# Between-products of all steps as 32x32x32 from the inverted blocks, and the first chunk's chain reordered without most fillers

## The chip, the cores and the metric

The kernel runs on one core of one Trainium2 chip. The metric is the device time of one execution, in microseconds. A core has TensorE (PE, with its weight loads shown apart as PEld), VectorE (DVE), ScalarE (ACT), GpSimd (POOL) and SyncE (SP), which here issues nearly all DMAs.

## The reference

A delta rule attention with 4 batches, 8 heads, 768 positions and head dimension 48, and behind it a feed-forward layer with a parametric ReLU.

```python
k_n = k / (norm(k) + 1e-06)
for t in range(S):                       # state: (B, H, 48, 48), from zero
    y[:, :, t] = q[:, :, t] @ state
    v_old = state^T k_n[:, :, t]
    state += beta_t * outer(k_n[:, :, t], v[:, :, t] - v_old)
x = y as (B*S, H*D) = (3072, 384)
h = x @ w_in                              # (384, 2048)
g = max(h, 0) + alpha * min(h, 0)
return g @ w_out                          # (2048, 384)
```

## The kernel before

**Tiling.** The sequence is cut into 12 chunks of 64 positions. A step n (24 of them) is one chunk of one pair of batches: two batches lie in the two halves of the 128 partitions, 8 heads along the free axis. Within a chunk the recurrence becomes a triangular system: the Gram matrix of k (grams) gives a unit triangular 64x64 matrix per batch and head, whose inverse is applied to the right-hand side (solve). Then come the outputs, the next state (next_state), and the transposes into the feed-forward's input (to_ffn).

**The inverse by blocks.** A 64x64 triangular matrix has two 32x32 diagonal blocks and one 32x32 block between them. The diagonal blocks of four steps at a time (NJ = 4) are inverted by DVE (eliminate; for the first four steps eliminate_small, which goes to 16 and lets TensorE do the last doubling in cross). Their results are `inverse` and its transpose `turned`. The off-diagonal block of the inverse is a product of three: inverse block, off-diagonal block of the Gram matrix (in `right`), inverse block. These are the between-products: between_1 multiplies `right` by the turned first block into `mid`, between_2 multiplies `mid` by the second inverse block, and the result goes into `inv`, from which solve reads. Partitions 0 to 31 and 64 to 95 hold first blocks, 32 to 63 and 96 to 127 second blocks.

In the kernel before there are two forms, chosen by `changes(n)` (n > 4):
- Steps 0 to 4: products of 64x64 weights and 32 columns per batch and head. The blocks are first copied with a mask (`which`, one column per block) into zero-padded 64x64 tiles `diag`; `right` and `mid` carry zero columns as well. DVE adds the result of between_2 to the second block (L720).
- Steps 5 to 23: products of 32x32 weights and 32 columns. For half of the heads the output is put in the other half of the partitions (`quad(2 * (t ^ a) + 1)`), so consecutive products use four places of the array; this takes second blocks copied across the partition halves (two 64x128 copies). ScalarE copies the result.

`place`/`placing` make these copies, with parts 0 (first block, turned), 1 (second block), 2 (into inv) and 3 (two small copies of weights).

**Order.** The order of every engine's instructions is the program's order; nothing is rescheduled. The start goes: statics (norms and Gram matrices of steps 0 to 3), queries, zeros (memzero of padded tiles on ScalarE), fillers (`busy(n)`: 2n products of 512 columns or part of one, whose result nobody reads, L1388), the elimination on DVE beside them, then first_chunk (steps 0 and 1 with nothing else to do on TensorE), second_pair (steps 2 and 3, woven with the first feed-forward products, first_in), and from step 4 on a steady mix: attention's bursts (burst_a, burst_b), with feed-forward products (L929 first layer, L971, L993 and later L1246 second layer) woven between by `weave`. In burst_b of step n, between_2 of step n + 1 and between_1 of step n + 2 share a call from step 7 on.

**Weights.** They come as 64-bit words in pieces of 512 KB. `fetch` issues a piece's DMA on SP, `begin` starts its conversion on ScalarE (L225, L226), the `conv_in` generator ends it on DVE in two parts (L235, L240) and then lets the next piece be fetched into the freed space. There are 12 pieces of w_in and six spaces. `convert(n)` runs n parts; `ahead[0]` tells how far `begin` may run ahead.

Names in the text: cross is L593 (first stage), L603 and L610 (second stage, with the copy L598 between); place is L648 on ScalarE and L644 on DVE; between_1 is L682 (32-wide) and L693 (64-wide), between_2 L707 and L712; their copies L689, L698, L725; solve L786 and L790; outputs L799; next_state L815 and L823.

Of the kernel before, what the change touches and what calls it, by code (L numbers as in the profile page):

```python
# [32 lines left out]
C = 64  # L33
HB = 32
W_IN_P = 512
BUSY = 8
# [7 lines left out]
def kernel(  # L44
# [272 lines left out]
    diag = [const.tile([128, H, C], FP32, name=f"diag{i}") for i in range(NE)]  # L317
    inv = [const.tile([128, H, C], FP32, name=f"inv{i}") for i in range(NE)]
    mid = [const.tile([128, H, C], FP32, name=f"mid{i}") for i in range(2)]

    right = [const.tile([128, H + 1, HB], FP32, name=f"right{i}") for i in range(EARLY)]

    def zeros():

        for t in right:
            nc.scalar.memzero(t[:, 0])
        for t in mid + diag + inv + state:
            nc.scalar.memzero(t)
# [89 lines left out]
    def grams(n, p=None):  # L418
# [10 lines left out]
        def weighted(dst, cols):  # L429
# [7 lines left out]
            lambda: weighted(right[n % EARLY][:, 1:], slice(HB, C)),  # L437
# [29 lines left out]
    def keep(n):  # L467

        m, j = n // NJ, n % NJ
        for t in range(2):  # L470
            own = slice(64 * t + HB, 64 * t + C)
            if n < FIRST + NJ and n != NJ - 1:
                nc.gpsimd.tensor_copy(out=same[m][own, j], in_=right[n % EARLY][own, 1:])
            elif n < NJ and t == 0:
                nc.vector.tensor_copy(out=same[m][own, j], in_=right[n % EARLY][own, 1:])
            else:
                nc.scalar.copy(same[m][own, j], right[n % EARLY][own, 1:])
# [144 lines left out]
    CROSS = 2  # L622

    def changes(n):

        return n > NJ

# [4 lines left out]
    def placing(n, parts, by_vector=False):  # L632
# [5 lines left out]
        first, second = slice(0, HB), slice(HB, C)  # L638

        def put(dst, cols, src, i, rows=slice(0, 128), to=None, a=slice(0, 2)):  # L640
            heads = slice(j * H + a.start * G, j * H + a.stop * G)
            out, x = dst[n % NE][to or rows, a.start * G : a.stop * G, cols], src[m][rows, heads]
            if by_vector:
                nc.vector.tensor_scalar(  # L644
                    out=out, in0=x, scalar1=which[rows, i : i + 1], scalar2=None, op0=ALU.mult
                )
            else:
                nc.scalar.mul(out, x, which[rows, i : i + 1])  # L648

        if 0 in parts:  # L650
            put(diag, first, turned, 0)
            yield
        if 1 in parts:
            put(diag, second, inverse, 1, a=slice(0, 1 if changes(n) else 2))
            yield
            if changes(n):
                for t in range(2):
                    put(diag, second, inverse, 1, half(t), half(1 - t), slice(1, 2))
                    yield
        if 2 in parts:  # L660
            put(inv, first, inverse, 0)
            yield
            if changes(n):
                put(inv, second, inverse, 1)
# [1116 lines left out]
```

## Time and profile before

| | |
|---|---|
| timed runs | 666.43, 671.92, 672.93 us, median 671.92 |
| profiled execution | 668.2 us, its span 666.5 |
| TensorE busy | 641.1 us (96%) |
| TensorE weight loads | 565.8 us (85%) |
| VectorE busy | 492.5 us (74%) |
| ScalarE busy | 288.6 us (43%) |
| GpSimd busy | 93.2 us (14%) |
| mean granted TensorE clock | 0.995 |

In the lines of the profile, a timeline row is start, length, engine, line, operation, written tile and read tiles, shape and count, and in brackets the idle time before it and what ended it. A row of the chain of waits is start, length, what. In the table of stages, each row is a stretch of time, its length, then for each of PE, PEld, DVE, ACT and POOL the busy time with the number of instructions, then the granted TensorE clock, the share of the DMA engines and GB/s. An fp32 product shows as two TensorE instructions. One between-call of a step is 16 products, so 32 instructions.

### The profile page before, as it was taken

What the parts mean: (1) busy time and instruction counts of PE and PEld (TensorE: products, weight loads), DVE (VectorE), ACT (ScalarE), POOL (GpSimd) and SP (SyncE); (2) the same over time, 40 slices, a digit from 0 to 9 for tenths busy, and PEclk for the clock granted to TensorE, in tenths of its full rate; (3) what the DMA queues carried; (4) which work ended last, traced back from release to release, by engine and by line L of the source; (5) the groups of instructions that cost most, each with busy time, mean ns of one, the idle gap of its engine ahead of it and who ended that gap; (6) DMA issues with size and microseconds to landing.
All of it is one profiled execution on the core that took longest, in us unless ns stands there. A gap on an engine that the chain in (4) does not pass through costs nothing.

```text
span 666.5 us, 22184 instructions
## 1 busy us (share of the span) xinstructions
PE 641.1 (96%) x9551; PEld 565.8 (85%) x9551; DVE 492.5 (74%) x1181; ACT 288.6 (43%) x675; POOL 93.2 (14%) x201
## 2 busy tenths in 40 slices
PE   4989999999998999999999999999999999999997
PEld 4577787666687998998998998998999999999997
DVE  5955889878989869748949747859869658568383
ACT  5837755336556343444434433324235345142140
POOL 6000121001010000001000000000035044053260
PEclk9799999999999999999999999999999999999999
DMA  8947754211332032122021022111112210100000
GB/s 121 243 120 200 192 115 120 72 36 32 68 74 49 11 65 50 21 53 49 15 49 36 15 48 37 20 44 36 27 37 38 37 36 5 25 14 2 24 1 25
DMA packets 110962, 37.72 MB, mean 57 GB/s; under 512 B 104160, under 2 KB 107248, under 8 KB 110864
## 3 DMA queue, kind: packets, MB, share of 16 engines
q1 hardware_dynamic: 109088, 35.81, 24.8%
q8 instruction: 75, 1.23, 0.8%
q10 hardware_dynamic: 1776, 0.49, 0.4%
q14 instruction: 23, 0.19, 0.1%
HBM read 31.56 MB, written 4.72 MB: 54 GB/s over the span
## 4 chain that ended last, share of the span: by engine, by line
PE 75%; DVE 15%; ACT 5%; issue 2%; SPq 2%; DMA 1%; POOL 0%; DVEq 0%; ACTq 0%; POOLq 0%
PE p_ffn L993 17%; PE p_ffn L929 16%; PE p_more L1246 8%; PE p_more L1161 4%; PE p_ffn L1151 3%; PE p_ffn L1246 3%; PE p_ffn L1156 2%; DVE prod L516 2%; DVE block L522 2%; PE p_pair L377 2%; PE p_pair L786 2%; DVE act L941 2%; PE p_pair L761 2%; PE p_pair L1388 2%; PE p_pair L799 2%
## 5 line engine op out<-in xcount | busy, mean ns | idle before, releaser
L929 PE MATMUL p_ffn<-xt,w_in 128*128 128x256 f32 x768 | 175.4, 383 | 5.0 <-ACT sums L939 1.8
L929 PEld LDWEIGHTS p_ffn<-xt,w_in 128*128 128x128 f32 x768 | 142.4, 190 | 26.3 <-ACT sums L939 2.2
L941 DVE SCALAR_TENSOR_TENSOR act<-act,al_t,p_ffn 128x256 f32<-128x256 f32 x112 | 48.6, 475 | 28.7 <-ACT act L939 28.6
L939 ACT ACTIVATE act<-p_ffn 128x512 f32<-128x512 f32 x56 | 33.3, 595 | 77.1 <-PE p_ffn L929 76.9
L522 DVE TENSOR_TENSOR block<-block,prod 128x30 f32<-128x30 f32 (+9 forms) x150 | 49.9, 333 | 5.1
L1185 POOL TENSOR_TENSOR k_t<-k_t 128x128 f32<-128x128 f32 (+1 forms) x48 | 29.6, 616 | 166.2 <-ACT k_t L1180 163.7
L516 DVE TENSOR_TENSOR prod<-block 128x30 f32<-128x30 f32 (+9 forms) x150 | 48.8, 326 | 3.3 <-POOL block L506 1.6
L993 PE MATMUL p_ffn<-w_out,act 128*128 128x192 f32 x288 | 49.6, 328 | 0.2 <-DVE act L941 0.2
L840 ACT COPY xt<-p_pair 128x384 f32<-128x384 f32 x22 | 10.4, 477 | 85.8 <-PE p_pair L838 73.6
L993 PEld LDWEIGHTS p_ffn<-w_out,act 128*128 128x128 f32 x288 | 46.5, 190 | 0.8 <-issue 0.5
L366 POOL TENSOR_TENSOR beta_t<-beta_t,rec 128x8 f32<-128x8 f32 x24 | 6.3, 261 | 291.1 <-DVE rec L364 270.8
L1185 POOL TENSOR_TENSOR block<-block 128x128 f32<-128x128 f32 (+1 forms) x48 | 28.0, 583 | 16.3 <-ACT block L1180 13.8
L1151 PE MATMUL p_ffn<-xt,w_in 128*128 128x256 f32 x96 | 28.7, 380 | 0.0
L648 ACT ACTIVATE diag<-inverse,which 64x128 f32<-64x128 f32 (+2 forms) x60 | 24.3, 404 | 2.3 <-DVE inverse L489 1.3
L771 DVE TENSOR_TENSOR r<-v_raw,p_pair 64x192 f32<-64x192 f32 (+1 forms) x66 | 23.2, 352 | 1.1
L725 ACT COPY inv<-p_pair 32x256 f32<-32x256 f32 x38 | 13.7, 362 | 23.6 <-DVE u L790 23.4
L790 DVE TENSOR_TENSOR u<-p_pair,wgt 128x384 f32<-128x384 f32 x24 | 13.3, 557 | 14.2 <-PE p_pair L682 10.1
L1200 DVE SCALAR_TENSOR_TENSOR act<-block,al_t,act 128x256 f32<-128x256 f32 x32 | 19.1, 638 | 5.2 <-ACT block L1196 5.1
L349 DVE TENSOR_REDUCE norm<-ksq 128x8 f32<-128x384 f32 x24 | 13.0, 545 | 12.9 <-ACT ksq L347 12.9
L1013 DVE TENSOR_TENSOR o_sb<-u,p_ffn 128x192 f32<-128x192 f32 x24 | 7.9, 352 | 19.7 <-PE p_ffn L993 19.2
L1246 PE MATMUL p_more<-w_out,act 128*128 128x192 f32 x128 | 21.9, 329 | 0.0
L1180 ACT COPY k_t<-p_more 128x512 f32<-128x512 f32 x16 | 9.4, 586 | 28.7 <-PE p_more L1161 25.9
(223 smaller groups left out, 1417.5 us busy)
## 6 DMA issues: line engine op xcount, KB each, us to landing
w_out<-in_moe_w_in_dram SPq DMA_DIRECT2D x12, 512.0 KB, 5.4
qp<-in_q_dram SPq DMA_DIRECT2D x48, 96.0 KB, 3.0
v_raw<-in_v_dram SPq DMA_DIRECT2D x48, 96.0 KB, 2.9
kl<-in_k_dram SPq DMA_DIRECT2D x96, 48.0 KB, 2.6
out_dram<-o_sb SPq DMA_DIRECT2D x92, 48.0 KB, 1.6
space_out<-in_moe_w_out_dram SPq DMA_DIRECT2D x11, 384.0 KB, 3.8
ke<-in_k_dram SPq DMA_DIRECT2D x43, 96.0 KB, 3.2
w_out<-in_moe_w_out_dram SPq DMA_DIRECT2D x5, 384.0 KB, 5.0
```

Source lines behind the costliest of these rows:

```text
L516: nc.vector.tensor_tensor(out=prod, in0=r[:, 0:j, j : j + 1].to_broadcast([128, j, n]), in1=r[:, j : j + 1, j + 1 : HB].to_broadcast([128, ...
L522: nc.vector.tensor_tensor(out=r[:, 0:j, j + 1 : HB], in0=r[:, 0:j, j + 1 : HB], in1=prod, op=ALU.add)
L648: nc.scalar.mul(out, x, which[rows, i : i + 1])
L771: nc.vector.tensor_tensor(out=r[to, a], in0=v_in[to, a], in1=p[own, a, :, 0:D], op=ALU.subtract)
L929: nc.tensor.matmul(p_h[:, i], w_in[:, t, (f + i) * 128 : (f + i + 1) * 128], xt[:, t], start=(t == 0), stop=(t == KT - 1),)
L939: nc.scalar.activation(g, p_h, ACT.Relu, scale=-1.0)
L941: nc.vector.scalar_tensor_tensor(out=g[:, i], in0=g[:, i], scalar=al_t[:, f + i : f + i + 1], in1=p_h[:, i], op0=ALU.mult, op1=ALU.add,)
L993: nc.tensor.matmul(p, x(i), w(i), start=(i == 0), stop=(i == FP - 1))
L1151: nc.tensor.matmul(p[:, f * 256 : f * 256 + 256], w(2, f), xt[:, 2], start=True, stop=False)
L1161: nc.tensor.matmul(q[:, j], a, b, start=True, stop=True)
L1185: nc.gpsimd.tensor_tensor(out=dst, in0=a, in1=b, op=ALU.add)
L1246: nc.tensor.matmul(p, x(i), w(i), start=(i == 0), stop=(i == FP - 1))
```

## The change

- All steps use 32x32x32 products. The first product goes from first-block rows to second-block rows of PSUM, the second from second-block to first-block rows, with no swap of halves. So a call that stands alone alternates between two places of the array; where between_2 of one step and between_1 of the next share a call, their products alternate head by head.
- between_1 reads `turned` itself for steps 0 to 3, and from step 4 a plain copy of it in `diag`; between_2 reads the second block out of `inv`. The masked copies into `diag`, the copies across halves, and the zero columns of `right`, `mid` and `diag` with their zero writes are gone. The result of between_2 is always copied, not added.
- placing yields 3 pieces instead of 6 (PLACING).
- statics: the transposes of step 0 (flips) go ahead of betas; weigh(0) ahead of squares(1).
- BUSY is 6 instead of 8; begin_in takes 5 pieces instead of 4 ahead of the elimination.
- first_chunk is rewritten: cross is written out with its two sums in banks of their own, one filler of 0.75 and one of 0.5 are left, placements and half of the copies go to DVE, and the masks, weight conversions, next-state updates and loads stand in another order: the loads of later k and v now come before the conversion of pieces 3 to 5.

```diff
-BUSY = 8
+BUSY = 6
...
-        for t in right:
-            nc.scalar.memzero(t[:, 0])
-        for t in mid + diag + inv + state:
+        for t in inv + state:
             nc.scalar.memzero(t)
...
+        own = slice(j * H, j * H + H)
+        def put(cols, i):
+            out, x = inv[n % NE][:, :, cols], inverse[m][:, own]
...
-        if 0 in parts:
-            put(diag, first, turned, 0)
+        if 0 in parts and n >= NJ:
+            nc.scalar.copy(diag[n % NE], turned[m][:, own])
             yield
         if 1 in parts:
-            put(diag, second, inverse, 1, a=slice(0, 1 if changes(n) else 2))
-            yield
-            if changes(n):
-                for t in range(2):
-                    put(diag, second, inverse, 1, half(t), half(1 - t), slice(1, 2))
-                    yield
+            put(slice(HB, C), 1)
+            yield
         if 2 in parts:
-            put(inv, first, inverse, 0)
-            yield
-            if changes(n):
-                put(inv, second, inverse, 1)
-                yield
+            put(slice(0, HB), 0)
+            yield
...
+    def turned_of(n):
+        return diag[n % NE] if n >= NJ else turned[0][:, n * H : n * H + H]
+
+    def products(n, second, p):
+        to, frm = (0, 1) if second else (1, 0)
+        x, y = (
+            (mid[n % 2], inv[n % NE][:, :, HB:C]) if second else (right[n % EARLY], turned_of(n))
+        )
+        def product(i, t):
+            rows = quad(2 * t + frm)
+            nc.tensor.matmul(p[quad(2 * t + to), i // G, i % G], x[rows, i], y[rows, i])
+        return product
+
+    def copied(n, second, p, vector=False):
+        to = inv[n % NE][:, :, HB:C] if second else mid[n % 2]
+        to = to.rearrange("p (a g) i -> p a g i", a=2)
+        def copies():
+            for t in range(2):
+                rows = quad(2 * t + (0 if second else 1))
+                if vector:
+                    nc.vector.tensor_copy(out=to[rows], in_=p[rows])
+                else:
+                    nc.scalar.copy(to[rows], p[rows])
+        return [copies]
+
+    def between(*wanted, vector=False):
...
+        for i in range(H):
+            for product in todo:
+                for t in range(2):
+                    product(i, t)
+        return [y for x in wanted for y in copied(*x, vector)]
...
-        soon += between_2(n + 1, b[:, :, WY : WY + G * HB])
+        wanted = [(n + 1, True, b[:, :, WY : WY + G * HB])]
         if n > JOINED:
-            soon += between_1(n + 2, b[:, :, 2 * WY : 2 * WY + G * HB])
+            wanted.append((n + 2, False, b[:, :, 2 * WY : 2 * WY + G * HB]))
+        soon += between(*wanted)
```

The new first_chunk from its second stage on, whole:

```diff
+        nc.scalar.copy(half_way[:, 0:bs, 0:LB], p)
+        begin_in(6)
+        busy(0.75)
...
+        for b in range(bs):
+            for i in (0, 2):
+                nc.tensor.matmul(
+                    one[quad(i), b], inverse[0][quad(i), b], half_way[quad(i), b, 0:LB]
+                )
+        for i in (0, 2):
+            y = turned[0][quad(i), 0:bs, 0:LB]
+            nc.vector.tensor_tensor(out=y, in0=y, in1=one[quad(i)], op=ALU.add)
+        for b in range(bs):
+            for i in range(4):
+                nc.tensor.matmul(
+                    two[quad(i), b], half_way[quad(i), b], inverse[0][quad(i), b, LB:HB]
+                )
+        scale_v(0)
+        y = inverse[0][:, 0:bs, LB:HB]
+        nc.vector.tensor_tensor(out=y, in0=y, in1=two, op=ALU.add)
         for i in both:
+            now(between_1(i, vector=i == 1))
+            place(i, (1,), True)
+        place(0, (2,))
+        place(1, (2,), True)
+        scale_v(1)
         for i in both:
+            now(between_2(i, vector=i == 1))
+        mask(0)
         for i in both:
             now(through_state(i))
             now(solve(i))
-        busy(0.5, ps_ffn())
+        mask(1)
+        busy(0.5)
         now(outputs(0))
+        state_of = [next_state(0)]
+        to_ffn(0, ps_ffn())
+        now(outputs(1))
+        state_of.append(next_state(1))
         convert(4)
+        to_ffn(1, ps_ffn())
+        convert(2)
         for i in both:
+            now(state_of[i])
             load_late(i + 2)
             load_v(i + 3)
+        convert(4)
         ahead[0] = FT * DM
         convert(2)
```

In second_pair the two calls of place(n, (0,)) are gone.

## The prediction

> **What bounds the kernel now.** I read the page's busy shares first, then the table of stages, the chain of waits up to 75 us, the timeline of the first 50 us, and last the rows of the between-product lines.
>
> ```profile
> PE 641.1 (96%) x9551; PEld 565.8 (85%) x9551; DVE 492.5 (74%) x1181; ACT 288.6 (43%) x675; POOL 93.2 (14%) x201
> 29.00:36.70 7.70, 7.52 (x331) 5.31 (x330) 5.61 (x15) 3.49 (x7) 0.00 (x0) 1.00 0.64 115
> 36.70:49.00 12.30, 10.30 (x333) 8.82 (x333) 6.93 (x16) 3.46 (x9) 0.00 (x0) 1.00 0.31 97
> 260.00:500.00 240.00, 239.77 (x3549) 220.47 (x3548) 178.19 (x437) 90.98 (x218) 11.14 (x25) 1.00 0.18 35
> ```
>
> From 260 to 500 us TensorE is busy for 239.77 of 240: there only TensorE work counts, and ScalarE (91 of 240) has slack. The first 49 us are different: TensorE is busy, but partly with products that compute nothing (L1388, the fillers), and those are on the chain that sets the end:
>
> ```profile
> 19.54 9.51 PE p_pair L1388 x16
> 29.04 1.33 PE p_pair L593 x89
> 30.37 1.06 PE p_pair L1388 x2
> 31.43 0.61 PE p_pair L603 x32
> 32.04 0.63 PE p_pair L1388 x2
> 32.67 0.61 PE p_pair L603 x32
> 33.28 0.63 PE p_pair L1388 x2
> 33.91 1.37 PE p_pair L610 x89
> ...
> 48.96 1.99 PE p_ffn L929 x8
> ```
>
> So 48.96, where the feed-forward products (L929) begin, is a chain's end, and every microsecond cut ahead of it is a candidate for the whole span. What DVE has ready, and when:
>
> ```profile
> 25.96 1.10 DVE L489 STREAM_TRANSPOSE turned<-block 128x256 f32<-128x256 f32 x2
> 26.92 2.22 DVE L489 STREAM_TRANSPOSE inverse<-block 128x256 f32<-128x256 f32 x4
> 36.18 0.42 DVE L619 TENSOR_TENSOR inverse<-inverse,p_pair 128x256 f32<-128x256 f32 x1
> 36.74 1.01 PEld L693 LDWEIGHTS p_pair<-diag,right 64*64 64x64 f32 x32 [0.41 <-ACT diag L648]
> 31.36 0.58 PEld L603 LDWEIGHTS p_pair<-act,inverse 32*32 32x32 f32 x32 [0.76 <-ACT act L598]
> 157.91 0.34 PEld L707 LDWEIGHTS p_pair<-diag,mid 32*32 32x32 f32 x32
> ```
>
> L593 could start at 27.06, when the turned blocks are there; the fillers hold it to 28.97. The last three rows are prices. A call is 32 instructions: 31.6 ns each for 64-wide products in two places of the array (L693), 18.1 for 32-wide ones with 16 columns in two places (L603), 10.6 for 32-wide ones with 32 columns in four places (L707).
>
> **What the skill says.** "TensorE: Matmul & The Clock Gate", Part 3, says that a weight load overlaps running products only where the row group differs. L707 uses two row groups, as L603 does, yet in four places it runs at 10.6 ns instead of 18.1; so I price by places. The same page, Part 1, describes a clock at half rate after an idle window of some 3.4 us and full after a busy one. The trace agrees in kind: 0.50 from about 17.2 to 24.3 us, after the idle stretch from 13.1 to 16.0, and 1.00 from then on. "ScalarE: Activation LUTs", What ACT_TABLE_LOAD costs, gives 186 ns + 0.833 ns per element, and 93 ns more for a per-partition operand: 492 for the masked 128x256 write, and the trace has 491 to 513 (L648). The plain copy that replaces one is then an estimated 400.
>
> **First chunk, step by step.** Times are of the profiled execution.
> Start: ScalarE drops 12 zero writes (right 1.05, mid 1.14, diag 1.14 = 3.3 us) and gets one weight piece more ahead of the chain (L225 + L226, 1.35), so it is free at 29.12 - 3.3 + 1.35 = 27.1. The pieces are there: the first six are issued between 14.76 and 17.94 and land within 8.4 us, by 26.3. The earlier transposes of step 0 can bring DVE forward by the wait for the step-0 Gram products, some 0.4 us at best; TensorE's fillers end later than that, so I count 0 (bounds -0.5 and 0).
> Fillers: BUSY 8 to 6 takes 4 products of 0.43: L593 at 27.25, ending at 28.6. In before the copy starts 1.68 after L593 does, so here it runs 28.95 to 29.3. The 0.65 us of filler left lies under that copy. The 64 products of "one" follow directly, 64 x 18.1 ns: 30.5 (before: 33.2, split by fillers). The 128 of "two" take 1.31: 31.8. DVE adds to turned 30.65 to 31.5 (L617, 2 x 0.42), scales v (0.55), and adds to inverse until 32.5. Before that was 36.60.
> Between-products: the new call has 32 instructions in two places with 32 columns. This isn't in the trace. From below L603's 18.1 ns (0.58 us), from above L693's 31.6 (1.01). L603 with 16 columns more, at the 0.84 ns per column of L1388 (0.43 us for 512), is 0.79 if nothing overlaps; I take 0.65. The first call for step 0 ends at 32.5, for step 1 at 33.2. Copies on ScalarE (2 x 0.365, L689) for step 0 end at 33.4; on DVE (2 x 0.42, as L617) for step 1 at 34.2, and step 1's inverse block, also by DVE, at 34.5. The second call for step 0 starts at 33.5, for step 1 at 34.6. ScalarE's copies end at 35.0, DVE's, behind two placements (0.35 each) and scale_v(1), at 36.25.
> Solve and output: DVE is now the slower side: mask(0) 0.75 to 37.0, u 2 x 0.56 to 38.1, mask(1) 0.75 to 38.9. The output products of step 0 run at 37.6, its y is copied by 38.8, its transposes wait for mask(1) (it reads both p_ffn banks); outputs(1) at 39.4, y by 40.6, transposes 40.65 to 41.1, xt copy 41.2 to 41.65. DVE converts three weight pieces (0.42 + 0.69 each) from 38.9 to 42.2, just ahead of the third product. So L929 starts at 41.7 for 48.96: -7.3 (bounds -5.0 and -8.5; a stall in TensorE's issue like the 0.59 ones at 37.9 and 45.7 would take part of it).
>
> **Second pair.** The first conversions end at 40.0 instead of 33.3, so weight pieces 6 to 8 are requested at 40 to 42.3, with 5.4 us to land. The last convert of the chunk puts piece 6 on ScalarE right after the xt copy at 41.65, where it waits for that landing until about 45; behind it stand squares(4), piece 7 and the two L598 copies, ready at some 48.6, and TensorE's L603 wants them at 41.7 + 6.8 = 48.5: just hidden, and each us that the landing is late is a us lost. SP then issues the 12 loads of k and v (10.2 us in before, 7.8 at 0.65 each) ahead of pieces 9 to 11, which before lay in front of the loads. Piece 9 lands at 56 to 58, L929's start plus 14.3 to 16.5. ScalarE wants it at plus 12, and in order behind it stand the L939 activations, the mid copies and the placements that the second between-call waits for (in before L712 waits there for ScalarE, 0.64 and 0.22). The two diag writes dropped (1.0) pay for the extra mid copies (1.46 for 0.62). ScalarE falls 2 to 4 us back, and has some 2 idle to win back: I take +1.5 on TensorE, less 0.3 for the shorter last product call: +1.2 (bounds 0 and +3.5).
>
> **Steps from 4 on.** Step 4: two calls at 0.65 for 1.01, -0.7. Calls that stand alone were in four places and now are in two: the first product of steps 5 to 8, the second of 5, 6, 7 and 23. Eight at 0.65 for 0.34: +2.5. In the 15 joint bursts the two calls alternate, so four places stay in turn: 64 instructions at 10.2 ns before (344.49 to 345.14) and after, 0 (bounds +-0.1 each). Sum +1.8 (bounds +0.8 and +5).
> ScalarE loses 0.40 + 0.81 + 0.1 us of placements in each of 19 steps, 25 us in all, beside TensorE work that hides it: I count -0.3 for L929's few waits on it (bounds -1 and 0). If that cover were missing it would be worth more, not less.
> Sum: -7.3 + 1.2 + 1.8 - 0.3 = -4.6 us. The profiled execution took 668.2 (span 666.5, 1.7 around it) and would take 663.6. The three timed runs are 666.43, 671.92, 672.93; the mean of all four is 670.0. The profiled one is no typical middle, so I subtract from the mean: 665.4.
>
> **The rivals.**
> A, the forecast: 665.4, chance 0.5.
> B, the head start is lost less: pieces 9 to 11 land in time and the two-place call costs 0.58. Then -7.3 + 0 + 0.8 - 1 = -7.5, 662.5. For it: DMA share is only 0.31 from 36.7 to 49. Against: SP issues in order. Chance 0.2.
> C, the gain is given back: the weight pieces land at the slow end, and two-place calls cost like L693: -5.5 + 3 + 4 = +1.5, 671.5; or an issue stall adds to the shorter chain. Chance 0.18.
> D, the other side: the clock. From 29.25 to 36.85 the new order has no full-array filler, 7.6 us of small products with gaps. If TensorE is throttled to half there, every microsecond of its work costs 0.5 to 1 more. Before, only a long filler stretch brought it back, and the next full-array stretch of over 5 us comes only after 90 us. It eats the 4.6 after some 10 us at half clock, and with 30 us at half clock it gives 670 - 5 + 15 = 680. For it: the half clock ended only within the fillers. Against: from 36.7 to 39.5 before, two products of 1.0 us with a 0.6 gap and no filler left it at 1.00. Chance 0.12.
>
> **How the numbers follow.** A and most of B and C give the range 659.5 to 671.5; the tail of D and a little of B are left out. About 1% (6.7 us) is what a measurement of this kernel can tell from no change. Below 665.2 lie B and almost half of A, 0.45; over 678.6 lies most of D, 0.1; the rest is 0.45.
>
> **What would show it.** Right: L593 near 27.2, L929's first near 41.7, clock 1.00 from 29 to 49, lone between-calls near 0.65 and joint bursts near 0.65 for 64. Wrong: a clock below 1.00 after 29 us; L929 starting after 44; a joint burst over 0.8; ScalarE waiting for a weight DMA between 50 and 60 us by more than 4 us.

## The result and the profile after

After takes 669.95 us (median of 19 executions, 667.72 to 671.85), before, on the same chip, 670.48 (19, 666.43 to 675.22). The ratio is 0.999 with the interval 0.9969 to 1.0011: no change that can be measured, where 665.4 was forecast. The profiled execution took 668.25 us, its span 666.5, to the tenth that of before.

Lines are renumbered: the first feed-forward products are L908 (L929 before), all between-products L671, their copies L686 on ScalarE and L684 on DVE, the placements L639 and L635, solve L765, outputs L778, next_state L794, the transposes into the feed-forward L817, the copy behind them L819, fillers L1368. The cross of the first chunk is L1402, then L1411 ("one") and L1419 ("two"). In kernels that keep before's first chunk on the new products the cross is L591, L601, L608.

The page's busy shares, and the three stages that were shown of before:

```profile
PE 642.7 (96%) x9535; PEld 569.2 (85%) x9535; DVE 494.3 (74%) x1180; ACT 263.1 (39%) x613; POOL 92.1 (14%) x201
29.00:36.70 7.70, 4.62 (x262) 3.81 (x264) 3.72 (x9) 2.85 (x6) 0.00 (x0) 0.88 0.50 90
36.70:49.00 12.30, 11.09 (x278) 9.19 (x275) 10.08 (x23) 2.83 (x7) 0.00 (x0) 0.52 0.36 106
260.00:500.00 240.00, 239.46 (x3550) 220.72 (x3549) 178.15 (x438) 78.67 (x191) 11.13 (x25) 1.00 0.18 36
```

ScalarE lost 25.5 us of work, as worked out. But in the first chunk TensorE, without the fillers, is busy for 4.62 of 7.70 us instead of 7.52, and from 36.7 on the granted clock is 0.52. The chain of waits through the chunk shows where the head start went:

```profile
26.54 1.10 DVE turned L487 x2
27.64 0.14 issue
27.78 1.39 PE p_pair L1402 x86
29.17 0.84 PE p_pair L1368 x2
30.01 1.08 PE p_pair L1411 x61
31.13 0.39 PE p_pair L1419 x38
31.51 0.80 issue
32.31 1.01 PE p_pair L1419 x62
33.33 0.71 PE p_pair L671 x44
34.04 2.28 issue
36.32 0.76 PE p_pair L671 x18
...
38.38 1.07 PE p_pair L671 x32
39.44 2.25 PE p_pair L765 x64
...
48.86 1.99 PE p_ffn L908 x8
```

Up to 31.5 the order does what was said. Then TensorE stops twice in the middle of a run of small products, 0.80 and 2.28 us, with nothing to wait for that the profile names ("issue"). After them the clock is halved: 32 instructions of L671 take 1.07 us at 38.38, and 0.69 at 143.03, at full clock. The table of stages, cut where the clock changes (its last three columns are the clock, the DMA share and GB/s):

```profile
31.51:34.79 3.28, 1.73 (x129) 1.58 (x128) 1.88 (x5) 0.86 (x3) 0.00 (x0) 1.00 0.48 86
34.79:41.60 6.81, 4.64 (x148) 4.33 (x147) 3.92 (x10) 1.10 (x3) 0.00 (x0) 0.50 0.31 58
41.60:48.43 6.83, 6.69 (x139) 5.09 (x136) 5.62 (x13) 1.54 (x4) 0.00 (x0) 0.50 0.41 137
```

That is 13.64 us at half clock, and L908 begins at 48.86 where before had 48.96. The clock falls again from 65.5 to 68.9 (behind 1.5 us of waiting for L615's turned block) and from 147.4 to 150.8. All of this lies on one grid: 13.64 is four times 3.41, and 65.5 is nine times 3.41 after 34.79. "TensorE: Matmul & The Clock Gate" in the Trainium skill, Part 1, gives such a free-running window, 3413 ns; the trace agrees. Before had only 6.8 us at half clock ahead of the end, from 17.6 on, and most of them lay under the fillers. A trace's clock counts as 1.00 ahead of its first record, which is at 24.55 in after. Its fillers up to there began 0.86 us apart, as those of before at half clock, so this part of the clock is the same in both and not in the 13.64.

How far each kernel is along is read from the start of DVE's u of each step (L790 before, L769 after), which takes up what solve gives, as a difference in us from before; "new products" is the experiment e_products below:

| u of step | before, us | after | new products |
|---|---|---|---|
| 0 | 42.82 | -1.7 | -0.9 |
| 2 | 83.98 | -1.0 | -1.4 |
| 4 | 157.57 | +0.2 | -0.8 |
| 5 | 174.80 | +0.5 | -0.6 |
| 9 | 268.45 | -0.2 | -1.2 |
| 13 | 369.49 | -1.0 | -2.1 |
| 17 | 467.39 | -1.0 | -2.1 |
| 18 | 492.69 | -0.2 | -2.0 |
| 23 | 606.20 | 0.0 | -1.8 |

### The profile page after: what moved, and what is told of

The parts are those of the page before. It is cut to its first block, busy times and chain, and to the rows that moved or that the text cites. A ratio compares the mean times of both kernels' runs of the same rounds, so it can differ in the third digit from the quotient of the medians.

```text
span 666.5 us, 22092 instructions
## 1 busy us (share of the span) xinstructions
PE 642.7 (96%) x9535; PEld 569.2 (85%) x9535; DVE 494.3 (74%) x1180; ACT 263.1 (39%) x613; POOL 92.1 (14%) x201
## 4 chain that ended last, share of the span: by engine, by line
PE 81%; DVE 11%; ACT 3%; issue 2%; DMA 1%; POOL 1%; SPq 0%; DVEq 0%; POOLq 0%; ACTq 0%
PE p_ffn L908 21%; PE p_ffn L972 17%; PE p_more L1225 8%; PE p_more L1140 4%; PE p_ffn L1130 3%; PE p_ffn L1225 3%; PE p_pair L375 3%; PE p_pair L671 2%; PE p_ffn L1135 2%; PE p_pair L740 2%; PE p_pair L765 2%; PE p_pair L778 2%; DVE prod L514 2%; PE p_pair L422 2%; DVE block L520 2%
## 5 line engine op out<-in xcount | busy, mean ns | idle before, releaser
L908 PE MATMUL p_ffn<-xt,w_in 128*128 128x256 f32 x768 | 176.3, 385 | 3.8 <-ACT sums L918 1.8
L908 PEld LDWEIGHTS p_ffn<-xt,w_in 128*128 128x128 f32 x768 | 143.8, 191 | 24.6 <-ACT sums L918 2.2
L920 DVE SCALAR_TENSOR_TENSOR act<-act,al_t,p_ffn 128x256 f32<-128x256 f32 x112 | 48.6, 475 | 29.0 <-ACT act L918 28.9
L819 ACT COPY xt<-p_pair 128x384 f32<-128x384 f32 x22 | 10.4, 478 | 91.3 <-PE p_pair L817 77.5
L686 ACT COPY inv<-p_pair 32x256 f32<-32x256 f32 x46 | 16.6, 361 | 26.9 <-DVE u L769 23.6
L769 DVE TENSOR_TENSOR u<-p_pair,wgt 128x384 f32<-128x384 f32 x24 | 13.2, 555 | 15.5 <-PE p_pair L671 14.8
L639 ACT ACTIVATE inv<-inverse,which 128x256 f32<-128x256 f32 x45 | 22.0, 504 | 1.7 <-DVE inverse L487 1.4
L1179 DVE SCALAR_TENSOR_TENSOR act<-k_t,al_t,act 128x256 f32<-128x256 f32 x32 | 21.7, 717 | 0.1
```

Source lines behind the costliest of these rows:

```text
L908: nc.tensor.matmul(p_h[:, i], w_in[:, t, (f + i) * 128 : (f + i + 1) * 128], xt[:, t], start=(t == 0), stop=(t == KT - 1),)
L920: nc.vector.scalar_tensor_tensor(out=g[:, i], in0=g[:, i], scalar=al_t[:, f + i : f + i + 1], in1=p_h[:, i], op0=ALU.mult, op1=ALU.add,)
L1179: nc.vector.scalar_tensor_tensor(out=g[:, f], in0=r[:, f], scalar=al_t[:, 2 * i + f : 2 * i + f + 1], in1=g[:, f], op0=ALU.mult, op1=ALU.add,)
```

## The experiments

The question was where 7.3 us of a shorter chain had gone. The theories, by the letters that the expectations use: F, TensorE waits for its own instructions, which arrive by DMA in packets, since small products use them up faster than they come. (One packet carries weight loads too, so each PE row of the profile counts for two.) Its rival Q: the stops come from the loads of k, v and q that the change moved in front. C: the clock falls because the fillers are gone. C was later sharpened to U: what fills a window of 3.4 us decides, and products on 32 rows do not count as work. The rows are those of the array that the weights take, the first number of a shape such as 32*128.

What made F worth trying is the row of the queue named "instruction" on the page of after (packets, MB, share):

```profile
q8 instruction: 75, 1.23, 0.8%
```

75 packets of 16 KB for 2 x 9551 TensorE instructions of before (2 x 9535 of after) are one for every 256. In after one starts at 33.49, and the stop ends at 36.32; in before one starts at 35.84, and the stop of 0.59 us that the prediction names ends at 38.46. A second sign is how many instructions lie ahead of a stop. From the start of the span to one of the stops in after, in before and in c_twice below:

```profile
0.00:34.03 34.03, 26.34 (x601) 18.46 (x602) 22.83 (x69) 21.00 (x47) 10.93 (x43) 1.00 0.83 178
0.00:37.85 37.85, 28.82 (x601) 19.14 (x601) 26.27 (x78) 24.36 (x59) 10.99 (x43) 0.91 0.86 183
0.00:36.08 36.08, 29.06 (x601) 19.40 (x601) 24.23 (x72) 23.51 (x58) 10.93 (x43) 1.00 0.83 178
```

All three stop behind PE row 601, though L671, L693 and L610 stand there. The other stops up to 46 us are behind rows 473 (after, b_quiet, j_busy8), 727 (e_products, k_mixed) and 855 (before, g_nolate, h_e_nolate, k_mixed). These counts are 126 to 128 apart, which is 252 to 256 instructions; a few records can be missing. A wait for data would move with the program.

**a_fill: fillers where the stops are**, in after: one ahead of "two", two ahead of the first between-products.

```diff
+        pause = ps_one()
-        busy(0.75)
+        busy(0.75, pause)
...
+        busy(1, pause)
...
+        busy(2, pause)
```

> The changed kernel with two fillers put back: one of 2 x 0.43 us between the first and the second set of chunk products, one of 4 x 0.43 us (1.7 us) ahead of the first between-call. Theory F (TensorE waits for its own instructions there, the idle time then halves its clock): the fillers take few instructions and stand where it waited, so the pauses of 0.80 and 2.28 us fall to under 1 us together, the clock stays at 1.00, the first feed-forward product starts at 44 to 45.5 us instead of 48.9, and the span falls by 3.5 to 4.5 us. Rival W (the pauses are a wait for data that the profile doesn't name): they stay, the fillers add 2.6 us, the clock holds, and the first feed-forward product starts at about 47.5; span -1.5 at most.

673.44 us (22 executions), ratio 1.0039 (1.0014 to 1.0065). The chain:

```profile
34.54 1.83 PE p_pair L1421 x128
36.37 3.64 PE p_pair L1368 x4
40.01 1.16 PE p_pair L671 x64
```

Both stops are gone: 128 instructions of "two" and then 64 of L671 run through, as F asks. But the clock had already fallen at 29.6, most of the fillers ran at half rate, which also slows the use of instructions, and L908 starts at 51.91, where 44 to 45.5 was expected. In this execution the first run of fillers met a full clock, ended at 25.1, and TensorE idled 2.77 us until the turned blocks came at 27.84. So a_fill says nothing on C.

**b_quiet: the loads back behind**, in after: ahead of the next-state updates of first_chunk.

```diff
-    load_v(2)
...
-    for i in range(2):
-        load_q(i + 2)
...
+        load_v(2)
+        for i in both:
+            load_q(i + 2)
```

> The changed kernel with the loads of v for step 2 and of q for steps 2 and 3 (6 DMAs, in flight from 31 to 37 us) moved behind the weight requests of the first chunk. Theory Q (the instructions come late because their DMA stands behind these loads): the pause of 2.28 us falls below 1.2, and if the clock only fell for the pause it stays at 1.00: first feed-forward product at 43 to 44.5, span -4 to -5. F without Q (the time of an instruction fetch is its own): the pause stays at 1.9 or more, the clock halves as before, first feed-forward product at 48.5 to 49.5, span within 1 us. Rival C (small products without fillers halve the clock, pause or no pause): the clock falls at 34 to 38 us even where the pause is gone.

675.73 us (7), ratio 1.0091 (1.0056 to 1.0126). The stops are 1.03 and 1.35 us, 2.4 together for 3.1. Most of this difference is not Q's: between the two stops the same instructions take 2.38 us for 1.73, because the clock is halved, and from the packet's start to the stop's end it takes 2.27 and 2.62 us for 2.31 and 2.83. So the loads have at most 0.2 us of a stop, and the stops stay. The clock fell at 30.6, a microsecond before the first stop, so a stop is not needed for the fall. The q loads themselves were then late: TensorE waited 3.4 us for them behind L908.

**c_twice: more small products in the old order.** In before, the 64 products of L610 in chunk one (128 PE rows) are issued twice:

```diff
-        for b in range(n):
+        for b in [b for _ in range(1 + (n > H)) for b in range(n)]:
```

> The kernel before, with the 128 products of the inverse update in the first chunk's cross (L610) issued twice into the same place; the result is unchanged. It adds 256 TensorE instructions, as many as one 16 KB instruction packet holds. F: the second set can't run faster than a packet comes, so L617's start moves by 2.3 to 2.8 us. W and C: by the array time alone, 1.3 us.

One execution, 679.28 us. The chain of waits, and then the queue's row:

```profile
34.46 1.63 PE p_pair L610 x106
36.09 2.53 issue
38.62 1.46 PE p_pair L610 x92
```

```profile
q8 instruction: 76, 1.25, 0.7%
```

128 more PE rows with their weight loads are 256 more instructions, and the queue has one packet more: a packet holds 256. One starts at 36.14 and the stop ends at 38.62: 2.5 us. The added products would take 1.4 us; L610 as a whole takes 5.6 (34.46 to 40.08) for 1.4 in before. That is 4.2 more, above the 2.3 to 2.8 that F gave: that figure had the stop alone, without the added products' own time and without the clock, which was 0.50 from 38.4 to 55.5, behind 2.4 us of idle time. With the stops at the same counts, F is shown, in an order that has none of the change.

**d_busy6: the shorter run of fillers alone.** In before:

```diff
-BUSY = 8
+BUSY = 6
```

> The kernel before with BUSY 6 for 8, nothing else. If the fillers only stand on the path, as the prediction has it, the first cross stage and the first feed-forward product both come 1.7 us earlier and the span falls by 1.7. F: part of it comes back as pauses of TensorE's issue between 30 and 47 us, because the same instructions must come in less time: the first feed-forward product moves by 0.5 to 1.2 us.

674.68 us (7), ratio 1.0089 (1.0054 to 1.0124). The prediction counted this cut at -1.7 us; it is +6 by the ratio, +4.5 by the medians (before has 670.21 here). The table of stages:

```profile
20.00:25.30 5.30, 5.30 (x24) 2.31 (x18) 4.63 (x19) 5.22 (x14) 0.00 (x0) 1.00 1.05 376
25.30:28.00 2.70, 0.35 (x1) 0.03 (x1) 2.42 (x9) 2.64 (x5) 0.00 (x0) 1.00 1.20 135
28.00:30.40 2.40, 2.40 (x130) 1.70 (x130) 2.40 (x6) 2.34 (x6) 0.00 (x0) 1.00 0.60 104
30.40:54.30 23.90, 23.90 (x526) 19.50 (x526) 10.48 (x26) 5.44 (x11) 0.00 (x0) 0.50 0.33 79
```

Twelve filler instructions at full clock take 5.42 us, not the 7.8 of an execution that starts them at half, and end 2.3 us before the cross starts. The window that ends at 30.46 has 0.9 us of this idle time and 1.5 of 32-row products; the clock falls to 0.50 and stays there for 23.9 us, fillers and all, to 54.36, 1.7 us ahead of L929. All seven executions took 673.2 to 676.1; that each had this gap is not shown. So the length of the fillers' run cannot be cut by a number read from one execution.

**e_products: the new products in the old first chunk.** All of the change's products and placements, but before's statics, first_chunk, BUSY = 8 and begin_in(4).

> The new products, placements and copies in all steps, but the first chunk, the statics, BUSY 8 and the four early weight pieces as in the kernel before: the change's first half alone. The prediction's terms, with the 0.58 us per lone call now seen in the changed kernel for its 0.65: steps 0 to 4 save 10 x 0.43 us of TensorE, of which some 1.7 in the first chunk and 2 later; eight lone calls cost 8 x 0.24 = 1.9: span -1 to -2.5 against before, if the fillers keep the clock (theory C, clock by fillers: 1.00 from 25 to 65 us). Rival P: the products themselves bring the losses (longer ScalarE copies ahead of waiting calls, the clock drop near 147 us that the changed kernel shows): span 0 to +3.

666.83 us (22), ratio 0.9956 (0.9932 to 0.9981): faster than before. After has 0.999 to the same before and was not run beside it. In the profile the cross starts at 27.14, 1.8 earlier than in before, because its fillers met a full clock, but L908 at 49.26: its chunk has a stop too, and a fall of the clock for two windows, 40.3 to 47.1, so its gain lies elsewhere (the table above). The gain is there at like clock too: its 7 executions with a mean clock of at least 0.994 have the median 665.7, the 34 of before on this chip 668.1. The chain:

```profile
39.21 0.66 PE p_pair L765 x26
39.87 1.45 issue
41.33 1.35 PE p_pair L765 x36
```

**f_spread: after with BUSY 8 and short fillers through the chunk**, so that neither idle time nor stops are left: ahead of "two", ahead of the between-products, behind each between-call, and ahead of outputs(1).

```diff
-BUSY = 6
+BUSY = 8
...
+        busy(0.5, pause)
...
+        busy(1.5, pause)
...
+            busy(0.5, big[0][:, 0])
...
+            busy(0.5, big[0][:, 0])
...
+        busy(0.5, big[0][:, 0])
```

> The changed kernel with BUSY 8 and with fillers spread over its first chunk: 0.43 us between the two sets of chunk products, 1.3 after them, 0.43 after each of the four between-calls and after the first transposes, so that no 3.4 us of it are without some; 3.9 us of fillers in all, of which some 3 lie in the pauses seen there. C (small products alone, or idle time, halve the clock; fillers among them hold it): clock 1.00 from 25 us on, first feed-forward product at 45.5 to 47 for 48.9, span 663.5 to 665.5 in the profile, ratio to before 0.992 to 0.998. Rival: the clock falls all the same between 28 and 48, and the first feed-forward product comes after 50.

673.92 us (22), ratio 1.006 (1.0035 to 1.0086). TensorE never idles between 28.9 and 51, there is no stop over 0.15 us, and still the clock falls at 34.34, at the end of a window with some 0.9 us of full-array filler and 2.5 of 32-row products. It then stays at 0.50 to 51.4, although from 37.5 to 46.1 half of the time is fillers (1.15 us beside 1.0 of L671, in turn). Idle time is thus not needed for the fall. (In after itself the window ahead of the fall had both: no filler, and 1.5 us of idle time.) L908 starts at 54.45.

**g_nolate: before without its three late fillers:**

```diff
-        busy(0.5, ps_ffn())
...
-        busy(0.5, ps_ffn())
...
-        busy(0.5, ps_ffn())
```

> The kernel before without the three fillers of 2 x 0.35 us in the second half of its first chunk (after the first between-calls, after solve, after next_state); all else as before. If fillers are only time on the path, as the prediction counted them, the first feed-forward product comes 1.5 to 2.1 us earlier and the span falls as much. C: the clock falls to 0.50 somewhere between 38 and 48 us without any pause of more than 0.7 us, the first feed-forward product is as late as before or later, and the span rises by 0 to 4.

667.99 us (22), ratio 0.9982 (0.9959 to 1.0004). The clock is 1.00 from 24.7 on, where its record begins, though from 34.3 on no filler is left; L929 starts 18.84 us after L593, before 19.99. C as it stood is wrong: without fillers, 64-row products hold the clock.

**h_e_nolate: the same three lines taken out of e_products**, so 32-row products where g_nolate has 64-row ones.

> The kernel e_products (new products and placements, first chunk of before) without its three late fillers of 2 x 0.35 us in the first chunk. With 64-wide products the same removal (g_nolate) left the clock at 1.00 and brought 1.15 us of chain. U (a window of about 3.4 us that holds only 32-wide products and idle halves the clock): from the 33.5 us filler on, the next 3.4 us hold only 32-wide between-calls and waits, so the clock falls between 37 and 42 and stays at 0.50 until the feed-forward products; L908 begins at 50 to 53 (49.26 with the fillers), time 667 to 670. Rival (width does not matter, only idle does): the clock stays at 1.00 as in g_nolate, L908 at 48.0 to 48.5, 665.5 to 666.5. F (instruction packets) expects one issue pause of 1 to 2 us among the solve products in both cases, earlier by the fillers that are gone.

667.15 us (14), ratio 0.9984 (0.996 to 1.0009). The windows of g_nolate first, then those of h_e_nolate:

```profile
37.74:41.15 3.41, 2.91 (x101) 2.80 (x98) 0.28 (x2) 1.55 (x4) 0.00 (x0) 1.00 0.19 70
41.15:44.56 3.41, 3.10 (x167) 2.85 (x166) 2.41 (x6) 0.46 (x1) 0.00 (x0) 1.00 0.02 5
```

```profile
37.74:41.15 3.41, 2.46 (x105) 2.00 (x106) 0.00 (x0) 2.49 (x8) 0.00 (x0) 1.00 0.55 161
41.15:44.56 3.41, 3.14 (x102) 2.98 (x106) 1.34 (x3) 1.10 (x3) 0.00 (x0) 0.51 0.02 5
```

The clock falls at 41.2, inside the range U gave, and comes back after one window, earlier than U said; solve's products, which fill it, are 64 rows high. The pair alone does not decide between rows and idle time, as TensorE also idles 0.45 us more in the first window; f_spread and m_width do. L908 starts at 48.19, not at 50 or later: from the cross to L908 it takes 19.02 us, g_nolate 18.84. U has the place and the sign, but one window at half clock is a small price here, and the new products don't gain in the chunk what they cost in clock.

**j_busy8: after with its old run of fillers:**

```diff
-BUSY = 6
+BUSY = 8
```

> After with BUSY 8 in place of 6 (two full-array fillers of 0.86 us in sum more ahead of cross), nothing else: separates the shorter filler stretch from the reordered chunk. F and U: the long stretch was not what failed; the chunk behind it has the same two issue pauses (about 0.8 and 2.3 us) and the same windows of 32-wide products, so the clock halves again at 34 to 36 and L908 starts between 48.5 and 51; time 669 to 673. Rival (the cut of BUSY alone starts the fall, as in before with BUSY 6, where the clock fell at 30.6): the clock holds until the feed-forward products, L908 at 43 to 45, 664 to 667.

670.48 us (14), ratio 1.0017 (0.9992 to 1.0042). Stops of 0.67 and 2.37 us, clock 0.50 from 34.0 to 44.3, L908 at 47.26. The shorter run of fillers is not what took the change's gain; the reordered chunk has both faults by itself.

**m_width: the clock measured by itself.** Ahead of before's fillers, ten products of 512 columns in a row, of various weights, between full-array fillers:

```diff
+    def narrow(frm, to, rows, n):
+        p = ps_one()
+        for i in range(n):
+            r, o = frm[i % len(frm)], to[i % len(to)]
+            nc.tensor.matmul(p[o:o + rows[1], 0:512], ident[r:r + rows[0], r:r + rows[1]], moving[r:r + rows[0], 0:512])
...
+    busy(12)
+    narrow((0,), (0,), (64, 64), 10)
+    busy(12)
+    narrow((0,), (0,), (32, 32), 10)
+    busy(12)
+    narrow((0, 64), (32, 96), (32, 32), 10)
+    busy(12)
+    narrow((0,), (0,), (32, 128), 10)
+    busy(12)
+    narrow((0,), (0,), (112, 32), 10)
+    busy(12)
```

> Measures the disputed cost by itself, without small instructions. Before with fillers only, ahead of its BUSY run: stretches of ten products of 512 columns each, issued back to back (20 instructions, so no instruction pauses and no idle), of 64x64, 32x32 in one place, 32x32 alternating between the two places of the change, 32 rows x 128 columns of weights, and 112 rows x 32 columns of weights; between them and around them twelve full-array fillers (112 x 128). Nothing is left out of the computation; the fillers' results are not read. U (the width counts, not only idle): the clock stays at 1.00 through the 64x64 stretch and falls to 0.50 within one or two windows of 3.4 us in the 32x32 stretches, although TensorE never idles; full-array fillers bring it back. What rows or columns alone do, no theory says. Rival (only idle counts): the clock stays at 1.00 from the first full stretch through all of them, and every product takes 0.86 us.

The timeline, in which these products are all L1538; the five stretches follow the order of the diff. Their shape column gives the weights (rows*columns), then the result:

```profile
30.17 8.79 PE L1538 MATMUL p_pair<-k_t,ident 64*64 64x512 f32 x20
49.39 13.27 PE L1538 MATMUL p_pair<-k_t,ident 32*32 32x512 f32 x20
75.33 4.48 PE L1538 MATMUL p_pair<-k_t,ident 32*32 32x512 f32 x20
90.23 13.31 PE L1538 MATMUL p_pair<-k_t,ident 32*128 32x512 f32 x20
116.25 8.77 PE L1538 MATMUL p_pair<-k_t,ident 112*32 112x512 f32 x20
```

The second stretch cut at the clock's fall:

```profile
49.39:53.45 4.06, 4.06 (x11) 1.08 (x11) 0.00 (x0) 0.00 (x0) 0.00 (x0) 1.00 0.00 0
53.45:62.66 9.21, 9.21 (x12) 1.62 (x10) 0.00 (x0) 0.00 (x0) 0.00 (x0) 0.50 0.00 0
```

TensorE is busy throughout, and after 4.1 us of 32-row products the clock is halved. With 32 rows and 128 columns the same, after 4.2 us. With 112 rows and 32 columns, or 64 rows, it stays at 1.00: rows count, columns don't. The rival, that only idle time counts, is out. Fillers brought the clock back 4.5 us after they began.

**n_share: pairs of places, and mixtures.** As m_width, with 36 products alternating between the change's two places, then fillers and 32-row products in turn:

```diff
+    narrow((0, 64), (32, 96), (32, 32), 36)
+    busy(12)
+    for _ in range(6):
+        busy(1)
+        narrow((0,), (0,), (32, 32), 2)
+    busy(12)
+    for _ in range(4):
+        busy(1)
+        narrow((0,), (0,), (32, 32), 4)
```

> As m_width (fillers ahead of the BUSY run, nothing left out), other stretches, with twelve full-array fillers around each: 36 products of 32x32x512 alternating between the two places of the change (72 instructions, some 16 us if pairs run at once as in m_width); then six times one full-array filler and two 32x32x512 products in one place (a third of the time full); then four times one full-array filler and four of the latter (a fifth full). In m_width 32-row products halved the clock 4.06 us after their start although TensorE never idled, 64-row and 112-row ones did not. If rows in use count, the pairs of the two-place stretch (64 rows at once) keep 1.00, and the clock stays 1.00 with a third of full filler and falls with a fifth. Rival (the narrow product's rows alone decide): the two-place stretch falls to 0.50 within two windows, like one place.

```profile
31.38 15.64 PE L1538 MATMUL p_pair<-k_t,ident 32*32 32x512 f32 x72
...
85.91 3.62 PE L1538 MATMUL p_pair<-k_t,ident 32*32 32x512 f32 x8
89.46 1.42 PE L1388 MATMUL p_pair<-k_t,ident 112*128 112x512 f32 x2
90.81 7.03 PE L1538 MATMUL p_pair<-k_t,ident 32*32 32x512 f32 x8
```

Two places at once (0.22 us each, half of the 0.44 of one place) hold the clock for 15.6 us, as rows in use ask. A third of full-array filler holds it too, a fifth does not: it falls at 90.16. After that fall two filler instructions in every 9 us don't bring it back. The real products of the change alternate between two places too, but with 16 or 32 columns each they overlap only in part: an instruction every 18 ns (32 weight loads in 0.58 us), where one of 32 columns at 0.84 ns has 27 ns of work, is an estimated 1.5 places or 48 rows. Those of 16 columns in "two" (128 weight loads in 1.31 us in before, so 13 ns of work every 10 ns) come to 1.3 places or 42 rows, and the waits between the calls come on top.

**k_mixed: both gains together?** g_nolate, with the change's products and placements where changes(n) holds, so from step 5 on:

```diff
-            put(diag, first, turned, 0)
+            if changes(n):
+                nc.scalar.copy(diag[n % NE][:, :, first], turned[m][:, j * H : j * H + H])
+            else:
+                put(diag, first, turned, 0)
...
+            put(inv if changes(n) else diag, second, inverse, 1)
```

> Before without the three late fillers (as g_nolate, 64-wide products for steps 0 to 4) and with the new products and placements from step 5 on. If the gain of e_products against before, about 1.2 us between steps 4 and 12 in the trace, comes from the new products of the steady part, it adds to g_nolate's 2.4 us of trace time: 3.0 to 3.6 us below before, ratio 0.9935 to 0.9960, clock 1.00 through the first chunk. Rival (e_products gained in the first chunk and the second pair only, the lone two-place calls cost the +1.8 us that I predicted): no faster than g_nolate, ratio 0.998 to 1.001.

667.16 us (14), ratio 0.997 (0.9944 to 0.9996). The clock is 1.00 through the chunk, L936 (its first feed-forward product) starts at 47.46, and between the u of step 5 and step 13 it gains 1.5 us on before: that part is as expected. In the trace the whole is only 0.8 below before's, not 3: 1.2 go lost between steps 2 and 4, 0.8 at step 18, where TensorE waits 0.5 us for DVE's o_sb, as in after. g_nolate, with before's products, has the same wait and loses 0.8 there too. So the expected 3.0 to 3.6 did not come, and it is not shown to beat e_products, which ran on another chip. What it does have is the clock: 13 of its 14 executions have a mean clock of at least 0.994, 20 of 35 of before on that chip.

## Why the prediction was wrong

**The first chunk, "-7.3 (bounds -5.0 and -8.5)", is the step that failed; it was about -0.1.** Against its working: L1402 starts at 27.78 for 27.25. The second call of step 1 starts at 38.38 for 34.6, 3.8 late, of which 0.5 are from the start and 3.1 from the two stops. From there to L908 it takes 10.5 us for 7.1: 3.4 more, all of it but the last 0.4 us at half clock. 3.8 and 3.4 are the 7.2 that are missing. The stop was in the text, as "a stall in TensorE's issue like the 0.59 ones", which "would take part of it". It was sized by the row that happened to show it, and the halved clock was put at nothing in the sum. The old chunk had such a stop because 256 instructions ran out, and spacing them with fillers kept it at 0.59 us; without the late ones, in g_nolate, the second stop is 0.97. In the new chunk "one", "two" and the first two between-calls are 512 instructions with their weight loads, that would run in some 3.6 us, and want two fetches of about 2.5 us each in a row.

**Rival D had the right mechanism and too small a chance, 0.12.** It named the stretch from 29.25 on without a full-array filler and its sign, "a clock below 1.00 after 29 us". The argument against it, that two products of 1.0 us with a gap and no filler left the clock at 1.00 before, compared 64-row products with 32-row ones (g_nolate, h_e_nolate, m_width). Its price of 680 assumed 30 us at half clock: the chunk had 13.6, of which a part lay under waits, and two later windows had 6.8 more. The other half, "an issue stall adds to the shorter chain", stood in rival C. The measured 669.95 is near the upper end of the range, where C put it, and by this route, not by late weight pieces.

**Fillers were counted as time on the chain.** BUSY 8 to 6, -1.7, is +6 in before (d_busy6, 674.68). Its profile shows a 2.3 us gap, because the fillers start at full clock. Only one of several phases of the clock was in the profile that was read.

**The transposes of step 0 ahead of betas, counted 0 (bounds -0.5 and 0), came out at about +0.5 in the one profile of after:** DVE's block transposes begin at 15.53 for 14.98, and the turned blocks are ready at 27.64 for 27.06. TensorE then did have nothing left to hide it. This was not tried by itself.

**The second pair, "+1.2 (bounds 0 and +3.5)", had the wrong sign:** from L908 to the u of step 2 after gains 0.9 us. ScalarE did wait for the weight pieces, 1.8 us up to 60.85 and 1.2 up to 64.26, though L908 is not early. But the sum had only TensorE's waits on ScalarE. Between 49 and 86 us TensorE waits in before 0.9 us for ScalarE and 1.9 in stops for its instructions; in after 0.6 for ScalarE's placement, 1.5 for L615's turned block, and not at all in stops. So the stops, which the sum did not have here either, may have turned the sign; this was not tried by itself. (Of pieces 9 to 11, which the text has in front of the loads in before, the last was requested at 60.61, behind them.)

**Steps from 4 on: right in the lone calls, wrong in ScalarE.** A lone call at full clock is 0.58 us (by its weight loads, as the prediction's prices are), between the 0.34 of four places and the 0.65 taken. (The text's 0.79 for "if nothing overlaps" is a slip: 32 instructions with 16 columns more at 0.84 ns are 0.43 us more, so 1.01. The forecast doesn't use it.) "-0.3 (bounds -1 and 0)" for ScalarE is -1.5: from the u of step 5 to that of step 13, after, e_products, h_e_nolate and k_mixed gain 1.46 to 1.49 each, some 0.4 in every second step; g_nolate, with before's products, gains 0.1. A row of it, of before:

```profile
298.57 0.60 ACT L939 ACTIVATE act<-p_ffn 128x512 f32<-128x512 f32 x1
307.48 0.69 DVE L444 TENSOR_TENSOR a_t<-p_pair,minus 128x512 f32<-128x512 f32 x1
308.22 0.65 PE L377 MATMUL p_pair<-ident,ke 128*112 128x128 f32 x4
```

and of e_products:

```profile
296.92 0.60 ACT L918 ACTIVATE act<-p_ffn 128x512 f32<-128x512 f32 x1
305.82 0.69 DVE L442 TENSOR_TENSOR a_t<-p_pair,minus 128x512 f32<-128x512 f32 x1
306.66 0.60 PE L375 MATMUL p_pair<-ident,ke 128*112 128x128 f32 x4
```

The u of that step starts at 294.82 and 293.58. ScalarE has fewer placements ahead of its activation, which starts 3.34 us after u instead of 3.75; DVE works behind it and is done with a_t 0.42 earlier; TensorE's transposes of the next k, which stand right behind a_t's end in before, start 0.32 earlier. So a slack engine was late by fractions of a microsecond at a hand-over that the sums of busy time don't show.

Against it stand, in after, +1.2 between steps 2 and 4: it has a third fall of the clock at 147.4, behind a wait of 1.4 us for the mid copy. But before waits there for 0.9 us on the mid copy and 0.9 on diag, and e_products has the wait of 1.4 too and loses only 0.5, so the wait is not the whole of it. And +0.8 at step 18, the wait for o_sb, which g_nolate shares, so the new products don't cause it. With all this the steps behind the second pair come out at +1.0 for a forecast of +1.5, for other reasons than those given. (The mean of the four times, from which the sum was subtracted, is 669.9, not 670.0.)

**What stays open.** Why k_mixed loses 1.2 us between steps 2 and 4, where its clock stays at 1.00, and why e_products loses only 0.5 there. Why g_nolate, h_e_nolate, k_mixed and after lose 0.8 at step 18, and before and e_products nothing. What brings a halved clock back. The exact share of rows at which a window counts as idle: it lies between a fifth and a third of full-array work beside 32-row products.

## What to carry to other kernels

A filler that computes nothing can do two jobs, holding TensorE's clock and giving its instructions time to arrive, so before one is cut, count for each 3.4 us window the rows in use and for each run of small products the instructions. A stall of half a microsecond in "issue" is to be priced by what causes it, not by its size in the one row that shows it. In a change of two halves, run each half alone: here the new products are worth 0.4% in the old order (0.2 to 0.7), and with the new order nothing of it can be measured.

## What the runs showed of the hardware

- TensorE's instructions come in packets of 256 (75 packets for 19,102, one more for 256 more), and a stop for one ends 2.3 to 2.9 us after the packet starts: 2.3 to 2.6 where the DMA engines were busy for at most 0.09 of that time (b_quiet, e_products, g_nolate, k_mixed), 2.5 to 2.9 where for half of it or more (after, before, c_twice, g_nolate, j_busy8). At 10 to 18 ns for a small weight load with its product, the 128 pairs of a packet last 1.3 to 2.3 us.
- Busy is not enough to keep the clock: products on 32 rows halve it after 4.1 and 4.2 us of unbroken work, whether they have 32 columns or 128, while 64 rows, 112 rows with 32 columns, and two places of 32 rows at once hold it. The page named above speaks of how busy TensorE was; no idle gap of a whole window was needed here.
- Once halved, the clock came back at the end of a window of full-array or 64-row work, but not of every one: after 3.4 us in h_e_nolate, after 23.9 in d_busy6, whose windows from 37.3 on held nothing else and no idle time.
- The times of before spread by the clock: of the 28 executions shared with a_fill, the 12 with a mean clock of at least 0.994 have the median 667.2, the 10 with 0.989 or less 672.6. All 19 of after lie between 0.974 and 0.990, as do all 14 of j_busy8 (0.975 to 0.985).
